# A turning product in halves, a decoding moved up, two decodes finished on another engine, and two smaller moves, in a retention, experts and gated-convolution kernel

## The chip, the cores and the metric

The kernel runs on 1 core of one Trainium2 chip. The metric is the device time of one execution in microseconds (us); lower is better. The core has five engines, each with its own instruction stream worked through in order: TensorE (PE; its weight loads are listed as PEld), VectorE (DVE), ScalarE (ACT), GpSimd (POOL) and SyncE (SP). They hand work to each other by semaphores. A `q` behind an engine's name marks an instruction of its sequencer, such as the issue of a DMA.

## The reference

Three layers follow one another, on 2 x 768 tokens of 512 columns.

```python
def _attn_ref(q, k, v):                       # 2 batches, 8 heads, 768 steps, 64 columns
    for t in range(S):
        state = gamma * state + einsum('bhd,bhe->bhde', k[:, :, t], v[:, :, t])
        y[:, :, t] = scale * einsum('bhd,bhde->bhe', q[:, :, t], state)

def _moe_ref(x, w_gate, w_local, w1, w2):     # 8 experts, 512 -> 1024 -> 512
    logits = x @ w_gate; local_gate = sigmoid(x @ w_local)
    for s in range(S):
        fresh_e = argmax(logits[b, s])
        e = fresh_e if s == 0 or local_gate[b, s] < 0.5 else prev_e
        p = softmax(logits[b, s])
        out[b, s] = p[e] * (maximum(x[b, s] @ w1[e], 0) @ w2[e])

def _moe2_ref(x, w_in, conv_w, w_out):        # 512 -> 1024 -> 512
    h = maximum(x @ w_in, 0)
    gate = sigmoid(conv over 3 tokens of h with conv_w)
    return (h * gate) @ w_out
```

`w_in`, `conv_w` and `w_out` arrive as 64-bit numbers, which the kernel itself turns into 32-bit ones.

## The kernel before, in words

The program is written by hand in the order in which every engine works. Its stages, with their times in the profiled execution:

**Attention, 0 to 61 us.** The 1536 tokens are cut into 12 tiles of 128. The step of the loop for tile `i` writes, in this order: `a_Z` (queries against the carried state, L362), the load of the next queries and keys, `a_X(i - 1)`, `logits` and `a_store` of the tile before, then `a_AV` (masked scores against the values, L374), `a_U` (the state, L396), and `a_S(i + 1)` (scores, L346). `a_X` (L406) is the turning product: it multiplies the attention's transposed result `xT` with `xw`, an identity of 128 columns with the 9 columns of the gates beside it, so that 137 columns come out with tokens on the partitions. There are four such products per tile, two into each of two banks. Each float32 product is two instructions in the trace. VectorE masks the scores (L352) and does the routing; ScalarE copies; GpSimd scales queries and values (L325, L332); SP loads three buffers ahead.

**Experts, 61 to 266 us** (`moe`). Weights are split into a high part (`whi`, ScalarE, L172) and a low part (`wlo`, VectorE, L181), and each product is made three times: high x high, low x high, high x low. A split unit is one such pair on 128x1024 numbers; behind its low part the next raw load is issued on SP. Tokens are gathered (`xg`, L611) and turned (`T`, with `xsh` on ScalarE, L584, and `xsl` on VectorE, L585). Experts 0 and 7 are done in two halves by `alone(e, half, ...)`, a generator that is advanced between other calls; experts 1 to 6 by `L1` (into `hh` and `hl`, L718 and L719) and `L2` (L744).

Two side works run in between:

- *Decoding.* Sixteen units of `w_in` and `w_out` (512 columns each) are turned from 64 to 32 bits. `dec_first` issues two ScalarE steps (L215, L216) on a loaded unit `draw`; `dec_second` does five VectorE operations (L218 to L224), two GpSimd ones (L226, L227, into `wdec`), and issues the next `draw` load on SP. `dec_first` finishes an open decoding first. The temporaries `dmag`, `df` and `ds` exist once; with `dec_first(mo)` the first two are `dmf` instead, in a ring of two.
- *The rest of the routing.* `route_rest` has five steps (L554 to L575) on 128x12 or 128x96 numbers: rows, `isov` to `posi`, `ex` with an exponential on ScalarE (L566), the reciprocal of its sum, and `G_all`. Each `next(rest, None)` does one.

`overflow` is a branch for tokens that no block holds. All engines pass it; what is written behind it can't run ahead of it.

**The joint between experts and the last layer, 245 to 266 us.** While `alone(7, 0)` and `alone(7, 1)` run on TensorE, the last two units are decoded, and the experts' results, stored by ScalarE as `ys` into `scr` (L689), are gathered back in token order by GpSimd (`c_gather`, L968), scaled with `G_all` (`c_scale`; VectorE L942, and ScalarE L944 for tile 4, whose buffer is `x_last`), turned by `c_T` (TensorE L950) and split (ScalarE L960, VectorE L963).

**The last layer, 266 us to the end.** `h2` (L993) and `o2` (L1045) keep TensorE busy; ScalarE and VectorE do the convolution and the gate.

Of the kernel before, what the change touches and what calls it, by code (L numbers as in the profile page):

```python
# [8 lines left out]
F32 = mybir.dt.float32  # L9
# [5 lines left out]
ALU = mybir.AluOpType  # L15
# [82 lines left out]
def tile_kernel(ctx: ExitStack, tc: tile.TileContext, consts, qk, kv, w1, w2, w_in, conv_w, w_out, out):  # L98
# [95 lines left out]
    n_dec = KD + KF // 2  # L194
    wdec = [(dp if j < n_dec - KEPT else cst).tile([P, 1024], F32, name=f"wdec{j}") for j in range(n_dec)]

    def decode(raw64, out, pool=None, s=None):

        n, m = out.shape
        r3 = raw64.rearrange("p (c two) -> p c two", two=2)  # L200
        lo, hi = r3[:, :, 0], r3[:, :, 1]

        def tmp(name, dt):
            return dp.tile([P, DM], dt, name=name, tag=name)[0:n, 0:m]

        if pool is None:
            mag, f = tmp("dmag", F32), tmp("df", F32)
        else:
            both = pool.tile([P, 2, DM], F32, name="dmf", tag="ow", bufs=2)
            mag, f = both[0:n, 0, 0:m], both[0:n, 1, 0:m]  # L210
        s = (tmp("ds", F32) if s is None else s[0:n, 0:m]).bitcast(I32)
        a = mag.bitcast(I32)
        ve = nc.vector

        nc.scalar.activation(out=mag, in_=hi.bitcast(F32), func=AF.Abs)  # L215
        nc.scalar.activation(out=f, in_=lo.bitcast(U32), func=AF.Copy, scale=2.0 ** -52)  # L216
        yield
        ve.tensor_scalar(mag, mag, F64_LOW, F64_HIGH, op0=ALU.max, op1=ALU.min)  # L218
        ve.tensor_scalar(a, a, 4, -2 ** 31, op0=ALU.logical_shift_left, op1=ALU.bitwise_xor)
        yield  # L220
        ve.tensor_scalar(s, hi, -2 ** 31, None, op0=ALU.bitwise_and)
        ve.scalar_tensor_tensor(out=a, in0=a, scalar=1, in1=s, op0=ALU.logical_shift_right, op1=ALU.bitwise_or)

        ve.tensor_scalar(s, a, -2 ** 23, None, op0=ALU.bitwise_and)  # L224
        yield
        nc.gpsimd.tensor_tensor(out=f, in0=f, in1=s.bitcast(F32), op=ALU.mult)  # L226
        nc.gpsimd.tensor_tensor(out=out, in0=f, in1=a.bitcast(F32), op=ALU.add)  # L227

    dec_src = []
    for dt in range(KD):  # L230
# [13 lines left out]
        queue.dma_start(out=t, in_=dec_src[u].bitcast(I32))  # L244
        dec_raw[u] = t

    def dec_first(pool=None, s=None):
        dec_second()
        u = dnx["run"]
        if u >= len(dec_src):  # L250
            return
        dnx["run"] += 1
        dec_raw["g"] = decode(dec_raw.pop(u), wdec[u // 2][:, (u % 2) * DM:(u % 2 + 1) * DM], pool, s)
        next(dec_raw["g"])

    def dec_second(queue=nc.sync):
        if "g" in dec_raw:
            for _ in dec_raw.pop("g"):
                pass
            dec_load(queue)  # L260
# [139 lines left out]
    def a_X(i):  # L400

        xT = xT_t.pop(i)
        x_t[i] = x2
        for p in range(NP):
            o = (p % 2) * P
            nc.tensor.matmul(x_t[i][p // 2][:, o:o + XN], lhsT=xT[:, p, :], rhs=xw[:, p, :],  # L406
                             start=(p % 2 == 0), stop=(p % 2 == 1), skip_group_check=True)

    def a_store(i):

# [192 lines left out]
    def moe(mo):  # L603
# [11 lines left out]
        def T(e, halves=(0, 1)):  # L615
            if e not in xs_t:
                xs_t[e] = (mo.tile([P, KD, CAP], F32R, name="xsh", tag="xsh", bufs=1),
                           mo.tile([P, KD, CAP], F32R, name="xsl", tag="xsl", bufs=1))
            for half in halves:
                sl = slice(half * P, (half + 1) * P)  # L620
                transposed(xg_t[e].pop(half), *(x[:, :, sl] for x in xs_t[e]))
# [73 lines left out]
        def L1(e):  # L695
            xh, xl = xs_t.pop(e)
            hh, hl = h_tiles(e)
            pb = [bank("b") if j < 3 else std for j in range(KF // 2)]
            for dt in range(KD):
                wh, wl = split[e * 8 + dt]  # L700
                if dt == 0:
                    dec_second()
                elif dt == 1:
                    next(rest, None)
                elif dt == 2:
                    dec_first(mo)
                for ft in range(KF):
                    o = pb[ft // 2][:, (ft % 2) * CAP + OFF:(ft % 2 + 1) * CAP]
                    fs = slice(ft * P, (ft + 1) * P)

                    for n, (a, b_) in enumerate(((wh, xh), (wl, xh), (wh, xl))):
                        nc.tensor.matmul(o, lhsT=a[:, fs], rhs=b_[:, dt, OFF:], start=(dt == 0 and n == 0 and ft % 2 == 0),  # L712
                                         stop=(dt == KD - 1 and n == 2), skip_group_check=True)
                    if dt == KD - 1 and ft % 2:
                        fp = ft // 2
                        dst = hh[:, 2 * fp:2 * fp + 2, OFF:]
                        pair = pb[fp].rearrange("p (a t) -> p a t", a=2)[:, :, OFF:]
                        nc.scalar.activation(out=dst, in_=pair, func=AF.Relu)  # L718
                        nc.vector.scalar_tensor_tensor(out=hl[:, 2 * fp:2 * fp + 2, OFF:], in0=pair, scalar=0.0,  # L719
                                                       in1=dst.bitcast(F32), op0=ALU.max, op1=ALU.subtract)  # L720
                split.pop(e * 8 + dt)
                if dt < KD - 1:
                    split_unit(nc.vector)
# [53 lines left out]
            pass  # L777
        rest = route_rest()
        for n, _ in enumerate(first):
            if n in (0, 1, 2, 5):  # L780
                split_unit(nc.vector)
            if n == 5:
                T(0, (1,))
            if n == 3:
                overflow(mo)
                gather(1)
            if n == 5:
                dec_first()
            elif n == 7:
                dec_second()  # L790
        for n, _ in enumerate(alone(0, 1, True)):
            if n == 0:
                dec_first()
            elif n == 1:
                dec_second()
            if n == 9:
                T(1, (0,))
            elif n == 11:
                T(1, (1,))
                gather(2)  # L800
# [10 lines left out]
        for n, _ in enumerate(alone(e, 0, False)):  # L811
            if n in (0, 8, 13):
                dec_second()
            elif n == 5:
                dec_first()
            elif n == 9:
                dec_first(mo, x0)
        raw0 = [dp.tile([P, 2, DM], F32, name="yg0", tag="draw", bufs=2) for _ in range(2)]
        ygs = [raw0[c // 2][:, c % 2, :] for c in range(4)] + [x_last.rearrange("p a t -> p (a t)"), x0]
        for c in range(NC):  # L820
# [2 lines left out]
        for n, _ in enumerate(alone(e, 1, True)):  # L823
            if 8 <= n < 12:
                c_scale(n - 8)
            if n == 7:
                window(1, [wp.tile([P, 1024], F32R, name="x2", tag=tag) for tag in ("whi", "whi", "wlo", "wlo")])
            if 10 <= n < 14:
                c_T(0, n - 10, "ab"[n % 2])
            if n == 12:  # L830
                c_scale(4)
            if n == 13:
                c_scale(5)

    def overflow(mo):
# [413 lines left out]
```

## Time and profile before

| | us |
|---|---|
| median of 3 timed runs | 410.25 |
| lowest and highest of them | 409.18, 411.04 |
| the profiled execution | 409.37 |
| its span (first to last instruction) | 407.6 |

| engine | busy us | share of the span |
|---|---|---|
| TensorE | 391.4 | 96% |
| VectorE | 286.8 | 70% |
| ScalarE | 246.6 | 60% |
| GpSimd | 117.8 | 29% |

The granted clock of TensorE was 0.996 over the span, where 1.00 is 2.4 GHz. TensorE is busy nearly everywhere, but its matmuls are pipelined, so that "busy" counts an instruction also while it waits behind the one before. What an instruction really takes is read from the distance between one's start and the next's. Of the other engines, only the places count at which TensorE waits for them. The chain of waits followed back from the last instruction lies on PE for 66% of the span, on DVE for 17%, on ACT for 6% and on DMA for 5%.

### The profile page before, as it was taken

How to read it: one execution, taken by the hardware profiler on the slowest of the kernel's cores; microseconds unless marked ns; L12 is line 12 of the kernel's file. 1: busy time of each engine (PE TensorE's matmuls, PEld its weight loads, DVE VectorE, ACT ScalarE, POOL GpSimd, SP SyncE). 2: the span in 40 equal slices, each digit the busy share in tenths (PEclk: the TensorE clock that was granted, in tenths of full speed). 3: DMA queues.
4: the chain of work that ended last, by engine and by line, in shares of the span. 5: the costliest groups of instructions: out<-in, count | busy, mean ns of one | idle time of the engine just before them, and what ended most of it. 6: DMA issues, size and time to landing. Idle time of an engine off the chain costs nothing.

```text
span 407.6 us, 7354 instructions
## 1 busy us (share of the span) xinstructions
PE 391.4 (96%) x2772; PEld 339.0 (83%) x2772; DVE 286.8 (70%) x544; ACT 246.6 (60%) x483; POOL 117.8 (29%) x110
## 2 busy tenths in 40 slices
PE   7999998979999999999999999799999999999996
PEld 4888876658989797998989777599979889998986
DVE  3368867957797999987877857659963736991350
ACT  4887752646855766576757563478864537981431
POOL 3455510264035153564744246532000000000000
PEclk9999999989999999999999999999999999999999
DMA  8999992868878797988979130533010010001002
GB/s 289 396 351 407 325 347 92 239 232 284 308 244 277 270 318 255 290 298 277 304 246 304 53 101 26 156 90 92 0 51 27 0 54 27 2 0 51 27 0 77
DMA packets 28087, 73.24 MB, mean 180 GB/s; under 512 B 3009, under 2 KB 3649, under 8 KB 28050
## 3 DMA queue, kind: packets, MB, share of 16 engines
q1 hardware_dynamic: 19506, 54.67, 39.1%
q10 hardware_dynamic: 6240, 10.55, 7.2%
q0 software_dynamic: 2304, 7.54, 6.0%
q8 instruction: 22, 0.36, 0.4%
q14 instruction: 15, 0.12, 0.1%
HBM read 62.26 MB, written 10.49 MB: 178 GB/s over the span
## 4 chain that ended last, share of the span: by engine, by line
PE 66%; DVE 17%; ACT 6%; DMA 5%; issue 4%; POOL 1%; ACTq 0%; DVEq 0%; POOLq 0%
PE c L1045 15%; PE b L993 11%; PE c L744 11%; DVE wlo L181 6%; PE rt L993 5%; PE b L712 4%; PE c L406 2%; PE b L652 2%; PE state L712 2%; PE rt L712 2%; PE b L346 2%; ACT whi L172 2%; DMA raw<-in_moe_w_dram 2%; PE a L374 2%; DMA C<-in_consts_dram 1%
## 5 line engine op out<-in xcount | busy, mean ns | idle before, releaser
L181 DVE TENSOR_TENSOR wlo<-raw,whi 128x1024 fp32r<-128x1024 f32 x64 | 82.1, 1295 | 18.4 <-ACT whi L172 17.6
L172 ACT CAST whi<-raw 128x1024 fp32r<-128x1024 f32 x64 | 66.7, 1055 | 40.6 <-PE c L744 21.9
L1012 DVE SCALAR_TENSOR_TENSOR cs<-hs,cw,cs 128x384 f32<-128x384 f32 x64 | 39.6, 619 | 30.6 <-ACT cs L1010 29.0
L226 POOL TENSOR_TENSOR dmf<-dmf,ds 128x512 f32<-128x512 f32 x12 | 24.9, 2076 | 83.5 <-DVE ds L224 50.1
L744 PE MATMUL c<-whi,hh 128*112 128x512 f32 x96 | 38.0, 395 | 0.3 <-ACT hh L718 0.3
L993 PE MATMUL b<-x,whi 128*128 128x386 f32 x176 | 37.1, 340 | 0.8 <-ACT x L960 0.8
L744 PE MATMUL c<-wlo,hh 128*112 128x512 f32 x96 | 37.5, 390 | 0.0
L1045 PE MATMUL c<-whi,gh 128*128 128x512 f32 x88 | 35.1, 399 | 0.0
L1045 PE MATMUL c<-whi,gl 128*128 128x512 f32 x88 | 34.9, 396 | 0.0
L1045 PE MATMUL c<-wlo,gh 128*128 128x512 f32 x88 | 34.7, 395 | 0.0
L993 PEld LDWEIGHTS b<-x,whi 128*128 128x128 f32 x176 | 31.2, 189 | 1.4 <-ACT x L960 1.2
L744 PE MATMUL c<-whi,hl 128*112 128x512 f32 x96 | 29.8, 392 | 0.6 <-DVE hl L719 0.6
L611 POOL DMA_INDIRECT xg<-scr,permi x15 | 20.3, 1353 | 26.5 <-DVE nbi L541 19.6
L712 PE MATMUL b<-xsl,whi 128*128 128x240 f32 x96 | 26.6, 277 | 0.4 <-DVE xsl L585 0.4
L712 PE MATMUL b<-xsh,whi 128*128 128x240 f32 x96 | 26.5, 276 | 0.0
L712 PE MATMUL b<-xsh,wlo 128*128 128x240 f32 x96 | 26.4, 275 | 0.0
L352 DVE TENSOR_TENSOR A<-b,mask 128x512 f32<-128x512 f32 x24 | 15.4, 685 | 11.1 <-PE b L346 11.1
L227 POOL TENSOR_TENSOR wdec<-dmf 128x512 f32<-128x512 f32 x13 | 22.8, 1757 | 1.0
L1016 ACT ACTIVATE sg<-cs 128x384 f32<-128x384 f32 x32 | 16.6, 519 | 9.1 <-DVE gl L1022 8.5
L744 PEld LDWEIGHTS c<-whi,hl 128*112 128x112 f32 x96 | 17.2, 181 | 5.8 <-DVE hl L719 1.5
L744 PEld LDWEIGHTS c<-whi,hh 128*112 128x112 f32 x96 | 17.4, 181 | 4.9 <-ACT hh L718 0.6
L744 PEld LDWEIGHTS c<-wlo,hh 128*112 128x112 f32 x96 | 17.4, 181 | 4.2
(251 smaller groups left out, 1015.9 us busy)
## 6 DMA issues: line engine op xcount, KB each, us to landing
raw<-in_moe_w_dram SPq DMA_DIRECT2D x64, 512.0 KB, 4.8
qk<-in_qk_dram SPq DMA_DIRECT2D x11, 512.0 KB, 6.6
kv<-in_kv_dram SPq DMA_DIRECT2D x11, 512.0 KB, 6.6
draw<-in_moe_w_in_dram SPq DMA_DIRECT2D x8, 512.0 KB, 3.6
draw<-in_moe_w_out_dram SPq DMA_DIRECT2D x8, 512.0 KB, 3.3
scr<-xo ACTq DMA_DIRECT2D x11, 256.0 KB, 8.1
out_dram<-os ACTq DMA_DIRECT2D x11, 256.0 KB, 2.0
scr<-ys ACTq DMA_DIRECT2D x10, 256.0 KB, 4.2
```

The costliest lines, as they stand in the source:

```text
L172: nc.scalar.copy(hi, raw[u])
L181: engine.tensor_tensor(out=lo, in0=t, in1=hi.bitcast(F32), op=ALU.subtract)
L226: nc.gpsimd.tensor_tensor(out=f, in0=f, in1=s.bitcast(F32), op=ALU.mult)
L227: nc.gpsimd.tensor_tensor(out=out, in0=f, in1=a.bitcast(F32), op=ALU.add)
L352: nc.vector.tensor_tensor(out=A_t[i][j], in0=sc2[j].rearrange("p (a t) -> p a t", a=NP), in1=mask.unsqueeze(1).to_broadcast([P, NP, P]), o ...
L611: nc.gpsimd.indirect_dma_start(out=t, out_offset=None, in_=xrow, in_offset=bass.IndirectOffsetOnAxis(ap=permi[:, col:col + 1], axis=0))
L712: nc.tensor.matmul(o, lhsT=a[:, fs], rhs=b_[:, dt, OFF:], start=(dt == 0 and n == 0 and ft % 2 == 0), stop=(dt == KD - 1 and n == 2), skip ...
L744: nc.tensor.matmul(yp[t][0:P - o], lhsT=a[:, ft, t * P + o:(t + 1) * P], rhs=b_[:, ws], start=(ft == 0 and a is hh and b_ is wh), stop=(ft ...
L993: nc.tensor.matmul(pb[:, 0:WN], lhsT=split[u_in + dt][wi][:, fs], rhs=x_[dt // 2][:, dt % 2, :], start=(n == 0), stop=(n == 3 * KD - 1))
L1012: nc.vector.scalar_tensor_tensor(out=cs, in0=tap[j], scalar=cw[:, j, ft:ft + 1], in1=cs, op0=ALU.mult, op1=ALU.add)
L1016: nc.scalar.activation(out=sg, in_=cs, func=AF.Sigmoid)
L1045: nc.tensor.matmul(ops[t][:, 0:n_], lhsT=a[:, ts_], rhs=b_[:, ws], start=(ft == 0 and n == 0), stop=(ft == KF - 1 and n == 2))
```

## The change

Five edits:

1. `a_X` makes each product as two: 64 columns of `xT` into the lower half of the partitions, then 64 into the upper half.
2. The first decoding after `overflow`: `dec_first` stands at step 3 of `alone(0, 0)`, not 5; `dec_second` at step 4, not 7; the split unit of step 5 at step 7. The turning `T(0, (1,))` stays at step 5.
3. `route_rest` is advanced in `L2` alone, so its five steps fall into experts 1 to 5 instead of 1 to 3.
4. The last two decodings end on VectorE: the operations of L226 and L227 leave GpSimd.
5. `c_scale(4)`, ScalarE's, stands behind `c_T(0, 3)` instead of ahead of it.

```diff
+    def decode(raw64, out, pool=None, s=None, last=nc.gpsimd):
...
-        nc.gpsimd.tensor_tensor(out=f, in0=f, in1=s.bitcast(F32), op=ALU.mult)
-        nc.gpsimd.tensor_tensor(out=out, in0=f, in1=a.bitcast(F32), op=ALU.add)
+        last.tensor_tensor(out=f, in0=f, in1=s.bitcast(F32), op=ALU.mult)
+        last.tensor_tensor(out=out, in0=f, in1=a.bitcast(F32), op=ALU.add)
...
         for p in range(NP):
             o = (p % 2) * P
-            nc.tensor.matmul(x_t[i][p // 2][:, o:o + XN], lhsT=xT[:, p, :], rhs=xw[:, p, :],
-                             start=(p % 2 == 0), stop=(p % 2 == 1), skip_group_check=True)
+            for half in HALF:
+                nc.tensor.matmul(x_t[i][p // 2][half, o:o + XN], lhsT=xT[:, p, half], rhs=xw[:, p, :],
+                                 start=(p % 2 == 0), stop=(p % 2 == 1), skip_group_check=True)
...
                 if dt == 0:
                     dec_second()
-                elif dt == 1:
-                    next(rest, None)
                 elif dt == 2:
                     dec_first(mo)
...
-            if n in (0, 1, 2, 5):
+            if n in (0, 1, 2, 7):
                 split_unit(nc.vector)
-            if n == 5:
-                T(0, (1,))
             if n == 3:
                 overflow(mo)
                 gather(1)
-            if n == 5:
                 dec_first()
-            elif n == 7:
+            elif n == 4:
                 dec_second()
+            elif n == 5:
+                T(0, (1,))
...
             elif n == 5:
-                dec_first()
+                dec_first(last=nc.vector)
             elif n == 9:
-                dec_first(mo, x0)
+                dec_first(mo, x0, nc.vector)
...
                 c_T(0, n - 10, "ab"[n % 2])
-            if n == 12:
+            if n == 13:
                 c_scale(4)
-            if n == 13:
                 c_scale(5)
```

In the order of instructions, TensorE in one tile of the attention before (`c_79` and `c_80` are X's two banks, `a_75` and `a_76` those of Z and A·V; x2 counts products):

```order
L362 MATMUL a_75<-qk,Z_106 64x128
L362 MATMUL a_76<-qk,Z_106 64x128
L406 MATMUL c_79<-xw,xT 128x137 x2
L406 MATMUL c_80<-xw,xT 128x137 x2
L374 MATMUL a_75<-A_300,kv 64x128 x2
L374 MATMUL a_76<-A_301,kv 64x128 x2
```

And the same tile with the change:

```order
L362 MATMUL a_75<-qk,Z_106 64x128
L362 MATMUL a_76<-qk,Z_106 64x128
L407 MATMUL c_79<-xw,xT 64x137 x4
L407 MATMUL c_80<-xw,xT 64x137 x4
L374 MATMUL a_75<-A_304,kv 64x128 x2
L374 MATMUL a_76<-A_305,kv 64x128 x2
```

Nothing moves; two products of a bank have become four, in the array shape that A·V has.

VectorE behind the branch of `overflow` before:

```order
L181 TENSOR_TENSOR wlo<-raw,whi 128x1024
L585 TENSOR_TENSOR xsl<-a_76,xsh 128x4x128
L218 TENSOR_SCALAR dmag<-dmag 128x512
L219 TENSOR_SCALAR dmag<-dmag 128x512
L221 TENSOR_SCALAR ds<-draw 128x512
L222 SCALAR_TENSOR_TENSOR dmag<-dmag,ds 128x512
L224 TENSOR_SCALAR ds<-dmag 128x512
L687 COPY ys<-c_79 128x512
```

And with the change:

```order
L218 TENSOR_SCALAR dmag<-dmag 128x512
L219 TENSOR_SCALAR dmag<-dmag 128x512
L221 TENSOR_SCALAR ds<-draw 128x512
L222 SCALAR_TENSOR_TENSOR dmag<-dmag,ds 128x512
L224 TENSOR_SCALAR ds<-dmag 128x512
L586 TENSOR_TENSOR xsl<-a_76,xsh 128x4x128
L181 TENSOR_TENSOR wlo<-raw,whi 128x1024
L688 COPY ys<-c_79 128x512
```

The five operations of the decoding have passed the split and `xsl`, and the split now follows `xsl`. On ScalarE the two steps of the decoding have likewise passed `whi` and `xsh`.

VectorE in the joint before (`x_108` is the buffer `x0`):

```order
L224 TENSOR_SCALAR ds<-dmag 128x512
L218 TENSOR_SCALAR dmf<-dmf 128x512
L219 TENSOR_SCALAR dmf<-dmf 128x512
L221 TENSOR_SCALAR x_108<-draw 128x512
L222 SCALAR_TENSOR_TENSOR dmf<-dmf,x_108 128x512
L224 TENSOR_SCALAR x_108<-dmf 128x512
L644 TENSOR_TENSOR hl<-a_75,hh 128x4x128
```

And with the change:

```order
L224 TENSOR_SCALAR ds<-dmag 128x512
L226 TENSOR_TENSOR df<-df,ds 128x512
L227 TENSOR_TENSOR wdec_93<-df,dmag 128x512
L218 TENSOR_SCALAR dmf<-dmf 128x512
L219 TENSOR_SCALAR dmf<-dmf 128x512
L221 TENSOR_SCALAR x_108<-draw 128x512
L222 SCALAR_TENSOR_TENSOR dmf<-dmf,x_108 128x512
L224 TENSOR_SCALAR x_108<-dmf 128x512
L226 TENSOR_TENSOR dmf<-dmf,x_108 128x512
L227 TENSOR_TENSOR wdec_93<-dmf 128x512
L645 TENSOR_TENSOR hl<-a_75,hh 128x4x128
```

Four operations have come to VectorE, two behind each decoding; on GpSimd the gathers of L968 now follow the decoding before these two directly.

## Rows read from the trace of the kernel before

**Rows 1.** Chain of waits: start us, us, what (a run of instructions counts as one).

```profile
11.67 1.14 PE c L406 x8
...
253.73 4.50 DMA yg<-scr,posi
```

**Rows 2.** Windows: stretch, length, busy (count) of PE, PEld, DVE, ACT, POOL; PEclk; DMA share; GB/s.

```profile
36.00:46.00 10.00, 9.75 (x160) 8.27 (x160) 9.31 (x30) 7.16 (x22) 5.22 (x8) 1.00 1.01 374
87.40:90.40 3.00, 3.00 (x8) 2.17 (x7) 2.61 (x3) 1.80 (x3) 2.43 (x2) 0.50 0.53 175
257.00:258.00 1.00, 0.00 (x0) 0.00 (x0) 0.00 (x0) 0.00 (x0) 0.70 (x2) 1.00 0.65 221
```

**Rows 3.** Timeline of PE in one attention tile: start us, us, engine, line, operation, tiles.

```profile
20.23 1.21 PE L406 MATMUL c<-xw,xT 128*128 128x137 f32 x8
21.37 1.09 PE L374 MATMUL a<-A,kv 128*64 128x128 f32 x16
22.29 0.63 PE L396 MATMUL state<-kv 128*64 128x64 f32 x16
```

**Rows 4.** Timeline of PE around the first decoding; in brackets idle before it, and releaser.

```profile
79.40 0.50 PE L652 MATMUL b<-whi,xsl 128*128 128x512 f32 x1
...
86.38 0.66 PE L640 MATMUL a<-ident,hr 128*128 128x128 f32 x4 [2.99 <-ACT hr L663]
```

**Rows 5.** Timelines of DVE, POOL and ACT around the first decoding.

```profile
77.52 1.23 DVE L181 TENSOR_TENSOR wlo<-raw,whi 128x1024 fp32r<-128x1024 f32 x1 [0.21 <-ACT xsh L584]
...
81.71 0.68 DVE L687 COPY ys<-c 128x512 f32<-128x512 f32 x1
...
83.33 1.26 POOL L227 TENSOR_TENSOR wdec<-df,dmag 128x512 f32<-128x512 f32 x1
...
84.62 0.66 ACT L215 ACTIVATE dmag<-draw 128x512 f32<-128x512 f32 x1 [5.98 <-POOL wdec L227]
```

**Rows 6.** Timelines of ACT and PE in experts 2 and 3.

```profile
128.37 0.28 ACT L566 ACTIVATE ex<-ex 128x96 f32<-128x96 f32 x1 [4.74 <-DVE ex L565]
...
132.20 0.48 PE L744 MATMUL c<-whi,hh 128*112 128x512 f32 x1 [0.34 <-ACT hh L718]
...
133.56 0.49 PE L744 MATMUL c<-whi,hl 128*112 128x512 f32 x1 [0.18 <-DVE hl L719]
...
156.89 0.48 PE L744 MATMUL c<-whi,hl 128*112 128x512 f32 x1 [0.45 <-DVE hl L719]
```

**Rows 7.** Timeline of POOL in expert 1, beside a split of VectorE.

```profile
117.59 2.15 POOL L226 TENSOR_TENSOR dmf<-dmf,ds 128x512 f32<-128x512 f32 x1 [19.93 <-issue]
```

**Rows 8.** Timelines of the joint: DVE, ACT, POOL and PE.

```profile
246.75 1.40 DVE L219 TENSOR_SCALAR dmf<-dmf 128x512 int32<-128x512 int32 x1
...
252.81 0.69 DVE L644 TENSOR_TENSOR hl<-a,hh 128x512 fp32r<-128x512 f32 x1 [2.04 <-ACT hh L643]
...
255.60 0.69 DVE L644 TENSOR_TENSOR hl<-a,hh 128x512 fp32r<-128x512 f32 x1 [0.61 <-ACT hh L643]
...
248.17 0.33 ACTq L689 DMA_DIRECT2D scr<-ys  x1
...
264.92 0.73 ACT L944 ACTIVATE x_last<-x_last,G_all 128x512 f32<-128x512 f32 x1
...
252.28 1.30 POOL L227 TENSOR_TENSOR wdec<-dmf 128x512 f32<-128x512 f32 x1
...
258.76 2.02 POOL L968 DMA_INDIRECT x_last<-scr,posi  x1 [0.30 <-issue]
...
258.79 0.66 PE L950 MATMUL a<-ident,yg 128*128 128x128 f32 x4 [2.46 <-DVE yg L942]
...
265.76 0.96 PE L993 MATMUL b<-x,whi 128*128 128x386 f32 x4 [0.81 <-ACT x L960]
```

**Rows 9.** Page, DMA issues: tiles, engine, operation, count, KB each, us from issue to landing.

```profile
out_dram<-os ACTq DMA_DIRECT2D x11, 256.0 KB, 2.0
scr<-ys ACTq DMA_DIRECT2D x10, 256.0 KB, 4.2
```

More of the change, by code (lines that the diff above doesn't have):

```diff
@@ L195, in tile_kernel @@
     wdec = [(dp if j < n_dec - KEPT else cst).tile([P, 1024], F32, name=f"wdec{j}") for j in range(n_dec)]
-    def decode(raw64, out, pool=None, s=None):
+    def decode(raw64, out, pool=None, s=None, last=nc.gpsimd):
         n, m = out.shape
@@ L245, in dec_load, with dec_first @@
         dec_raw[u] = t
-    def dec_first(pool=None, s=None):
+    def dec_first(pool=None, s=None, last=nc.gpsimd):
         dec_second()
@@ L252, in dec_first @@
         dnx["run"] += 1
-        dec_raw["g"] = decode(dec_raw.pop(u), wdec[u // 2][:, (u % 2) * DM:(u % 2 + 1) * DM], pool, s)
+        dec_raw["g"] = decode(dec_raw.pop(u), wdec[u // 2][:, (u % 2) * DM:(u % 2 + 1) * DM], pool, s, last)
         next(dec_raw["g"])
```

## The prediction, made before the result

> **What bounds the kernel now.** I read the chain of waits first, then the timelines of the stretches that the edits touch, and the windows last. The profiled execution took 409.37 us, of which the span is 407.6. From about 266 us to the end, TensorE is dense in the output network and no edit reaches that far, so whatever is won or lost before 266 us arrives at the end in full. The question is who ends last in five places.
>
> In the attention the turning product (X, line 406) is itself on the chain in eight of the eleven tiles that the loop turns (the first of these pieces stands in [rows 1]). In the other three, around 32 to 47 us, VectorE is busy 9.31 of 10 us and the DMA engines are full (share 1.01) [rows 2]. In the mixture of experts TensorE is dense with four kinds of exception: 2.99 us before 86.38 for ScalarE's relu `hr` [rows 4], three short waits in experts 2 and 3 [rows 6], 2.46 us before 258.79 for the first gathered rows, and 0.81 us before 265.76 for a cast [rows 8].
>
> **1. X in halves.** Four products of 128x137 (eight instructions, since each float32 product is two) become eight products of 64x137, sixteen instructions. X takes 1.14 us now, from 20.23 to 21.37. The nearest row is A·V right behind it: also eight products on 64 columns, sixteen instructions of 128 elements, in 0.92 us (21.37 to 22.29) [rows 3]. Scaled by 137/128 that is 0.985 us, so 0.155 us less per tile. Each of A·V's instructions starts 0.0575 us after the one before, which is only possible if the two halves run side by side. Eight tiles on the chain give 8 x 0.155 = 1.24 us. In the three tiles bound by VectorE I count nothing, and I round to **-1.3** for X and A·V having one array shape less between them. Bounds: 0, if loads become the bound at once, and -1.7, if all eleven tiles gain.
>
> X's sixteen rows are about as long as A·V's, so A·V already carries whatever the issue of twice the instructions costs. The Trainium skill, "TensorEngine Tiling (Array Packing)", section "Instruction Overhead", speaks against this edit: about 60 cycles of overhead for each matmul, and the advice not to take the tiling from a dimension that is already small. As an estimate from that page, eight more instructions at 60 cycles of 2.4 GHz are 0.2 us a tile, more than the gain, and the sum would be 1.3 us smaller by it; A·V's 0.0575 us for a whole instruction [rows 3] is why I don't go by it.
>
> **2. First decoding moved up (77 to 97 us).** Now the second decode's first ScalarE step (84.62) waits 5.98 us for GpSimd's `wdec` of the first (83.33 + 1.26) [rows 5], and the relu that TensorE needs stands behind it on ScalarE. Hence TensorE's 2.99 us [rows 4]. Afterwards the granted clock is 0.50 from 87.4 to 90.4 [rows 2], the 1.2 GHz level; the same products at 2.4 GHz would take half of those 3.0 us, so the slow clock costs 1.5 us.
>
> In the changed order VectorE runs the five decode operations ahead of `xsl`, and the split `wlo` (1.23) behind it. The five now lie between the end of `xsl`, just before TensorE's product on it at 79.40 [rows 4], and `ys` at 81.71 [rows 5]: about 2.35 us. `xsl` is then 2.35 - 1.2 = 1.15 us later, and TensorE waits that long at this product: a new wait of about 1.2 us. GpSimd starts about as much earlier as the split and `xsl` no longer stand ahead of the decode, 1.8 us, but the moved `wlo` now runs beside its two steps, and beside such a VectorE operation a GpSimd step took 2.15 us [rows 7] instead of 1.30 [rows 8]. So `wdec` is ready 0.7 to 1.7 us earlier, and TensorE goes on at 84.7 to 85.7 instead of 86.38; I take 85.2, **-1.2** net of the new wait, which lies inside it. Two waits of about 1.2 and 0.5 us then stand for one of 2.99. After a wait of 2.46 us the clock was still 1.00 [rows 2, 8], so I expect it to hold: -1.5. Against that, ScalarE does one `whi` ahead of the next relu, which I put at +0.3 to +0.5. Sum **-2.2**. Bounds: 0 (the wait only changes its place and the clock falls anyway) and -3.2 (1.7 + 1.5). SP's one raw load now stands behind the draw load, and the moved split unit is for expert 1, whose products begin only after 96 us: nothing.
>
> **3. Routing's rest later.** The step with the exponential sits on ScalarE at 128.37 after a wait of 4.74 us, and the splits and `hh` of expert 2 are behind it; the products for it waited 0.34 and 0.18 us, those of expert 3, where the last step runs ahead of two splits on VectorE, 0.45 us [rows 6]. In the new order no step stands in L1, so both neighbours disappear from those places. All three waits go: **-1.0**. The steps then land in experts 4 and 5, where TensorE does not wait. Bounds: 0, if a step in expert 2's L2 delays the same splits, and -1.3, with the restart after each wait.
>
> **4. Last two decodes finished by VectorE (tail).** The first gather (GpSimd) starts at 253.73 because `wdec` runs to 253.58, lands 4.50 us later [rows 1, 8], VectorE scales, TensorE turns at 258.79. After the change GpSimd is free, and the gather waits only for what it reads: the store of `ys`, issued 248.17 [rows 8]. Stores of this size landed in 2.0 or 4.2 us by the medians of two such stores [rows 9], so the gather can start between 250.2 and 252.4 and land between 254.7 and 256.9. Next late is then VectorE's order: the scaling stands behind `hl` at 255.60 + 0.69 [rows 8]. That puts TensorE at about 256.8: **-1.95**; with the slow store, which the gather's rows reach 0.6 us later, -1.3. The four operations added to VectorE are of the shape of `hl` (two inputs, 128x512), 0.69 us [rows 8], together 2.8 us. One of its decode operations now takes 1.40 us beside GpSimd and would shorten, and the 2.04 us in which it idles before 252.81 cover most of the rest [rows 8]. Without the shortening, 0.7 us of it would fall on the `hl` at 252.81.
>
> **5. One scaling behind the casts.** ScalarE's 0.73 us on `x_last` (264.92) stands ahead of the casts for which TensorE waits 0.81 before 265.76 [rows 8]. Moved behind them, the cast can start as soon as its transposes allow: **-0.55**; bounds 0 and -0.73. The store of `ys` behind it starts a little later, and nothing reads it soon.
>
> **Sum.** -1.3 - 2.2 - 1.0 - 1.95 - 0.55 = -7.0 us, 402.4 by the profiled execution. The median of the three timed runs is 410.25, 0.9 higher, which would make 403.25. I take the middle, **402.8 us**.
>
> **Rivals.**
> A. *Attention bound by its loads.* For it: a DMA share of 1.01 over ten microseconds [rows 2]. Against: X is on the chain in eight tiles with TensorE busy before and after. It takes part 1 away: 404.1.
> B. *The first decoding only trades its wait*: the clock falls again, or `xsl` costs what `hr` gave back. For it: the new wait of 1.2 us is certain by the order. Against: both waits together are shorter than the one now. Takes part 2 away: 405.0.
> C. *Gathers late.* The issue of the gather at 258.76, beside a VectorE split, took 2.02 us [rows 8], and the four new VectorE operations stand just ahead of the first gather. The Trainium skill, "SBUF — State Buffer", section "SBUF: two separate sides", has a rule by which this would come: VectorE and GpSimd share a port pair as an exclusive lock, and GpSimd that is locked out cannot write the descriptors of its DMAs; the 2.02 us agrees with it. Two new operations of 0.69 that hold the first gather up, and the slow store, cost 1.4 us, over half of part 4: 404.2.
> D. *Slower: the halves of X do not run side by side.* Then sixteen instructions of 1.14/8 = 0.1425 us take 2.28 us, 1.14 more per tile, in eight to eleven tiles +9.1 to +12.5, against 5.7 of the other parts: 413.7 to 417.1 by the median. It decides from 0.7 us more per tile. For it: nothing but that X's operand is wider. Against: A·V [rows 3].
> That an edit does nothing is no case of its own: the order of instructions shows all five.
>
> **Chances.** The forecast 0.62 (400.5 to 404), A 0.08, B 0.10, C 0.08, two or three of these together 0.07 (405.5 to 410, counted as within 0.5%), D 0.05. A difference under 0.5% (2.05 us, from 408.2 to 412.3) is about what a measurement of this kernel can't tell from no change; nearly three parts must fail for it. All bounds together reach from -9.3 (1.7 + 3.2 + 1.3 + 2.4 + 0.7) to 0; against the median that is 401.0 at the low end, against the lower profiled execution 400.1, and upward the range takes in A, B, C and the nearer half of their pairs: 400.0 to 406.3. Faster 0.88, same 0.07, slower 0.05.
>
> **What would show it.** Part 1: X at about 0.99 us per tile, the first A·V that much closer. Part 2: TensorE waiting about 1.2 us for `xsl` near 78 us and under 1 us for `hr`, and no slice at 0.50. Part 3: no wait over 0.1 us on `hh` and `hl` in experts 2 and 3. Part 4: first gather before 252.5 minus the earlier gains, TensorE waiting under 1 us for it. Part 5: the wait before the first output product under 0.3 us. Wrong would be X above 1.14 us, a clock of 0.50 in 80 to 90 us, or a new wait for VectorE between 110 and 235 us.

## The result: 404.63 us, and the profile after

The changed kernel takes 404.63 us (median of 4 runs, 404.07 to 404.94) against 409.72 us of the kernel before in the runs beside it. The ratio is 0.9875, with a 95% interval from 0.9856 to 0.9893: 5.1 us faster, where 7 were forecast. The sign and the range held; the gain was a quarter smaller. The result lies just outside the forecast's own bin (400.5 to 404).

Where it went is read from the starts of the same products in TensorE's two timelines. The table gives the distance between such starts, in us, in the profiled executions (409.37 and 404.4); what the prediction expected stands in the last column:

| stretch | before | after | difference | forecast |
|---|---|---|---|---|
| start to last tile's X | 60.76 | 60.79 | 0.0 | -1.3 (part 1) |
| to expert 1's first product | 35.93 | 33.73 | -2.2 | -2.2 (part 2) |
| experts 1 to 3 | 70.30 | 69.51 | -0.8 | -1.0 (part 3) |
| experts 4 to 6, and to the first turned `hr` of expert 7 | 72.17 | 72.50 | +0.3 | 0 |
| to the first output product | 26.60 | 24.20 | -2.4 | -2.5 (parts 4, 5) |
| to the last product | 138.39 | 138.46 | +0.1 | 0 |

**X in halves**, the timeline of PE in the tile of [rows 3]:

```profile
19.98 1.16 PE L407 MATMUL c<-xw,xT 128*64 128x137 f32 x16
20.98 1.09 PE L374 MATMUL a<-A,kv 128*64 128x128 f32 x16
21.85 0.34 PE L396 MATMUL state<-kv 128*64 128x64 f32 x5
```

X takes 1.00 us from its start to A·V's, as forecast (0.985), and A·V 0.87 instead of 0.92. The two halves do run side by side, and the overhead per instruction that the prediction set aside does not show. And yet the last tile's X starts when it did.

**The first decoding**, PE, DVE and POOL, against [rows 4, 5]:

```profile
80.73 0.50 PE L653 MATMUL b<-whi,xsl 128*128 128x512 f32 x1 [1.30 <-DVE xsl L586]
...
85.53 0.66 PE L641 MATMUL a<-ident,hr 128*128 128x128 f32 x4 [0.82 <-ACT hr L664]
...
80.59 1.99 DVE L181 TENSOR_TENSOR wlo<-raw,whi 128x1024 fp32r<-128x1024 f32 x1
...
81.58 2.16 POOL L227 TENSOR_TENSOR wdec<-df,dmag 128x512 f32<-128x512 f32 x1
```

Two waits of 1.30 and 0.82 us stand for the one of 2.99. The split and GpSimd's step beside it stretch each other, from 1.23 and 1.26 us [rows 5] to 1.99 and 2.16. The clock, in the window of [rows 2] (same columns), stays at its upper level:

```profile
87.40:90.40 3.00, 2.95 (x18) 2.21 (x17) 2.47 (x3) 2.25 (x4) 2.92 (x2) 1.00 0.46 146
```

**Experts and joint**, PE and POOL, against [rows 6, 8]:

```profile
153.93 0.49 PE L743 MATMUL c<-whi,hl 128*112 128x512 f32 x1 [0.36 <-DVE hl L718]
...
248.44 1.46 POOL L965 DMA_INDIRECT yg<-scr,posi  x1 [8.48 <-DVE dmf L226]
...
254.10 0.33 PE L947 MATMUL a<-ident,yg 128*128 128x128 f32 x1 [0.41 <-DVE yg L939]
...
260.73 0.44 PE L990 MATMUL b<-x,whi 128*128 128x386 f32 x1 [0.20 <-ACT x L957]
```

The waits of expert 2 are gone; that of expert 3 has stayed, at 0.36 for 0.45 us. The first gather now starts 5.3 us earlier (248.44 for 253.73), of which 2.6 us are the lead that TensorE already has at expert 7's first turned `hr` (236.53 for 239.16). TensorE waits 0.41 for its rows instead of 2.46, and 0.20 instead of 0.81 for the cast.

### The profile page after: what moved, and what is told of

Its sections match the earlier page's. It is cut to its first block, busy times and chain, and to the rows that moved or that the text cites. A ratio compares the mean times of both kernels' runs of the same rounds, so it can differ in the third digit from the quotient of the medians.

```text
span 402.6 us, 7552 instructions
## 1 busy us (share of the span) xinstructions
PE 388.7 (97%) x2868; PEld 336.9 (84%) x2868; DVE 295.2 (73%) x548; ACT 245.9 (61%) x483; POOL 111.5 (28%) x106
## 4 chain that ended last, share of the span: by engine, by line
PE 53%; DVE 13%; DMA 6%; issue 4%; ACT 3%; POOL 0%; ACTq 0%; DVEq 0%
PE c L1042 15%; PE b L990 12%; PE c L743 8%; DVE wlo L181 7%; PE rt L990 5%; DMA raw<-in_moe_w_dram 5%; PE b L711 3%; PE b L653 2%; ACT whi L172 2%; DVE hl L718 2%; DMA xg<-scr,permi 1%; PE c L672 1%; PE state L711 1%; PE rt L711 1%; DVE xsl L586 1%
## 5 line engine op out<-in xcount | busy, mean ns | idle before, releaser
L181 DVE TENSOR_TENSOR wlo<-raw,whi 128x1024 fp32r<-128x1024 f32 x64 | 87.1, 1381 | 12.0 <-ACT whi L172 11.3
L172 ACT CAST whi<-raw 128x1024 fp32r<-128x1024 f32 x64 | 66.6, 1057 | 41.0 <-PE c L743 18.9
L226 POOL TENSOR_TENSOR dmf<-dmf,ds 128x512 f32<-128x512 f32 x12 | 24.9, 2075 | 83.5 <-DVE ds L224 59.6
L227 POOL TENSOR_TENSOR wdec<-dmf 128x512 f32<-128x512 f32 x12 | 20.7, 1722 | 0.9
```

The lines of the kernel that those rows point to most:

```text
L172: nc.scalar.copy(hi, raw[u])
L181: engine.tensor_tensor(out=lo, in0=t, in1=hi.bitcast(F32), op=ALU.subtract)
L226: last.tensor_tensor(out=f, in0=f, in1=s.bitcast(F32), op=ALU.mult)
L227: last.tensor_tensor(out=out, in0=f, in1=a.bitcast(F32), op=ALU.add)
```

## The experiments

Theories: **(add)** the five parts add up as the prediction's sum has them; **(load)** rival A, the attention's loads take X's gain; **(DVE)** VectorE takes it between 30 and 47 us; **(chain)** the parts in the middle depend on each other, since expert 2's splits start from a raw load that doesn't come earlier with TensorE.

All profiles answer to one table, distances of starts in us as above (the way from the first X to the last is split at the 1st, 5th, 9th and 12th tile's X; what lies ahead of the first X, 11.5 to 11.9 us, is left out). Each row is one execution:

| kernel | X 1 to 5 | X 5 to 9 | X 9 to 12 | to expert 1 | experts 1 to 3 | 4 to `hr` of 7 | to output |
|---|---|---|---|---|---|---|---|
| before | 18.10 | 18.24 | 12.82 | 35.93 | 70.30 | 72.17 | 26.60 |
| after | 17.55 | 18.87 | 12.62 | 33.73 | 69.51 | 72.50 | 24.20 |
| x_only | 17.55 | 19.03 | 12.62 | 34.63 | 71.80 | 72.18 | 26.41 |
| dec_only | 18.10 | 18.23 | 12.82 | 33.65 | 71.10 | 72.17 | 26.82 |
| rest_only | 18.10 | 18.24 | 12.82 | 35.92 | 68.68 | 72.53 | 26.33 |
| no_rest | 17.56 | 18.19 | 12.64 | 33.56 | 71.44 | 72.18 | 24.20 |
| tail_only | 18.10 | 18.25 | 12.82 | 34.57 | 70.29 | 72.17 | 24.80 |
| scale_only | 18.09 | 18.37 | 12.82 | 35.90 | 69.71 | 72.17 | 26.04 |
| no_x | 18.10 | 18.24 | 12.82 | 33.66 | 69.20 | 72.48 | 24.18 |
| l2_dve | 17.56 | 18.37 | 12.62 | 33.87 | 68.64 | 72.17 | 24.33 |
| few_kv | 18.10 | 18.24 | 12.82 | | | | |
| few_kv_x | 18.72 | 18.05 | 12.62 | | | | |
| no_lo | 18.09 | 18.09 | 12.81 | 35.23 | 70.14 | 72.17 | 26.46 |
| no_lo_x | 17.56 | 18.29 | 12.62 | 36.42 | 71.04 | 72.17 | 26.50 |

### X in halves: x_only and no_x

x_only is the kernel before with the first edit alone:

```diff
-            nc.tensor.matmul(x_t[i][p // 2][:, o:o + XN], lhsT=xT[:, p, :], rhs=xw[:, p, :],
-                             start=(p % 2 == 0), stop=(p % 2 == 1), skip_group_check=True)
+            for half in HALF:
+                nc.tensor.matmul(x_t[i][p // 2][half, o:o + XN], lhsT=xT[:, p, half], rhs=xw[:, p, :],
+                                 start=(p % 2 == 0), stop=(p % 2 == 1), skip_group_check=True)
```

> The kernel before with the halves of X alone. The prediction's term expects -1.3 us (408.4 where before is at 409.7). Its rival A, attention bound by loads, expects X at 0.99 us per tile in the trace and yet 0.0, within 0.3 us, since GpSimd's scaling waits for the same loads at about 46.7 us as before. If the halves cost something where small products stand ahead of X (0.33 us has become 0.42 there), at most +0.3.

Measured: 409.56 against 409.51 us, ratio 0.9997 (0.9981 to 1.0014). no_x is the changed kernel without that edit (the same diff turned round).

> The changed kernel with X as four whole products again. The prediction's term expects it 1.3 us slower, 405.9. If the gain is lost within the attention, as the halves alone showed: 404.6, within 0.4 us, and if the halves gain in those executions in which no load is late, up to 0.7 us slower.

Measured: 404.02 us, ratio to before 0.9865 (0.9850 to 0.9881), where the changed kernel has 0.9875 (0.9856 to 0.9893). So the halves are worth nothing that can be measured, alone or with the rest. The table's first three columns say why: where whole products stand, the three stretches are 18.1, 18.1 to 18.4 and 12.8 us in every profile. Halves give 0.55 in the first (but for few_kv_x, below) and 0.20 in the last. In the middle the stretch is between 0.2 us shorter and 0.8 longer than before, which can take all of it back. The interval of x_only reaches to 0.8 us faster: it leaves out the -1.3 of part 1, but not a gain of some tenths in the executions whose middle is short (from the first X to the last 48.39 us in no_rest and 48.55 in l2_dve, against 49.16 before, 49.04 in the changed kernel and 49.20 in x_only).

### What takes it back: few_kv, few_kv_x, no_lo, no_lo_x

few_kv leaves out three of the attention's loads; few_kv_x has X in halves besides.

```diff
+FEW = (4, 6, 8)
...
+        if i in FEW:
+            kv_t[i] = kv_t[i - 1]
+            return
         t = ld.tile([P, 2, H, D], F32, name="kv", tag="kv", bufs=3)
...
     def a_scale_v(i):
-        if i >= NT:
+        if i >= NT or i in FEW:
             return
```

> The kernel before, but tiles 4, 6 and 8 of the attention take the keys and values of the tile before instead of loading and scaling their own (three loads of 512 KB less; the attention's result is another one). If the loads bind the attention: the last tile's X starts well over 1 us before 60.8. If VectorE binds it between 30 and 47 us: within 0.3 us of 60.8. The total depends on how the other result is routed, so only the pair with the next kernel is compared.

> The same with X in halves. If the loads took the gain of the halves, and no longer bind here: 0.8 to 1.6 us before few_kv, at the last tile's X and in the total. If VectorE or the end of the attention took it: the same as few_kv within 0.3 us.

The window of the middle tiles in few_kv (columns as in [rows 2]) and its last tile's X on PE:

```profile
36.00:46.00 10.00, 9.73 (x162) 8.28 (x160) 9.31 (x30) 6.01 (x18) 4.74 (x7) 1.00 0.87 317
...
60.80 0.38 PE L410 MATMUL c<-xw,x_last 128*128 128x137 f32 x1 [0.39 <-ACT x_last L387]
```

The DMA share falls from 1.01 to 0.87 and nothing moves: 60.80 for 60.76. So leaving out three loads gains nothing: they do not bind the kernel **before**. With halves on top the middle stretch gives 0.19 us, the best of all profiles, but its first stretch is 1.2 us longer than with halves elsewhere, of which 0.55 is a pause of TensorE at 26.1 us that nothing in the profile explains; the totals are equal (467.9 and 468.01 us, both long because the other result is routed into the `overflow` branch, whose products stand near 84 us in both profiles).

no_lo takes the splits from VectorE instead:

```diff
             t, hi = raw.pop(u), split[u][0]
+            if not load:
+                split[u] = (hi, hi[:, :])
+                return
             lo = wp.tile([P, 1024], F32R, name="wlo", tag="wlo")
```

> The kernel before without VectorE's five low-part splits during the attention (1.22 us each; the products with these low parts take the high part instead, so the first weights are less exact). Leaving out three loads had moved nothing in the attention. If VectorE binds the stretch from 30 to 47 us: the last tile's X starts 2 to 3.6 us before 60.8, until TensorE or the loads become the bound. If it was TensorE or the loads all the while: within 0.3 us of 60.8.

> The same with X in halves. If VectorE's splits took the gain of the halves in the middle tiles: 0.9 to 1.4 us before no_lo at the last tile's X, of it some 0.5 in the first five tiles. If the loads take it as soon as VectorE does not: 0 to 0.4 us, and GpSimd waiting over 1 us for queries between 30 and 50 us.

```profile
36.00:46.00 10.00, 9.92 (x162) 8.37 (x162) 6.73 (x27) 7.16 (x22) 4.38 (x8) 1.00 1.00 387
...
60.60 0.50 PE L409 MATMUL c<-xw,x_last 128*128 128x137 f32 x2 [0.38 <-ACT x_last L386]
```

VectorE falls from 9.31 to 6.73 us busy and the last X comes 0.15 to 0.2 us earlier. So VectorE, busy as it was, held up next to nothing: the chain of waits had shown its splits there, but TensorE is busy 9.75 of 10 us with them [rows 2] and 9.92 without. In time no_lo has 0.9979 (0.9967 to 0.9992) and no_lo_x 0.9984 (0.9968 to 1.0000) of the kernel before: the halves give nothing here either. Both theories that I had of the middle tiles fall for the kernel before. With halves, though, waits appear there or grow (the only one before is 0.25 us for VectorE's logits, at 40.33), in no_lo_x for ScalarE's copies (first two rows), in the changed kernel for VectorE's logits and in both for late loads (POOL):

```profile
32.79 1.20 PE L410 MATMUL c<-xw,xT 128*64 128x137 f32 x16 [0.25 <-ACT xT L386]
36.83 0.67 PE L365 MATMUL a<-qk,Z 64*64 64x128 f32 x16 [0.38 <-ACT Z L401]
```

```profile
40.55 0.34 PE L478 MATMUL rt<-ident,far 1*128 1x1 f32 x3 [0.85 <-DVE LG L441]
...
37.55 1.28 POOL L325 TENSOR_TENSOR qk<-qk,wdec 128x512 f32<-128x512 f32 x1 [1.44 <-DMA qk<-in_qk_dram]
```

By these waits TensorE, the loads, VectorE and ScalarE end there within some tenths of each other, so that a shorter TensorE meets the next at once. With halves the middle stretch is 18.05 us where loads were left out (few_kv_x), 18.2 to 18.4 in no_rest, no_lo_x and l2_dve, and 18.9 to 19.0 in the changed kernel and x_only. GpSimd's waits for loads between 28 and 40 us go with it, but don't order it: 4.3 us in the changed kernel, 1.9 in x_only, 2.9 in l2_dve, 0.4 before. What orders it is where a late load puts GpSimd's scaling of the queries. Where that runs beside a short step of VectorE, the step ends only after it, and TensorE waits for it or for what follows (0.35 us at 31.91 in x_only, 0.85 at 40.55 in the changed kernel). DVE and POOL of x_only, then DVE of the changed kernel, whose POOL row stands above:

```profile
30.34 1.51 DVE L507 TENSOR_SCALAR sl<-slot,R 128x256 f16<-128x256 f16 x3
...
29.75 1.27 POOL L325 TENSOR_TENSOR qk<-qk,tq 128x512 f32<-128x512 f32 x1 [1.67 <-DMA qk<-in_qk_dram]
...
38.19 0.68 DVE L218 TENSOR_SCALAR dmag<-dmag 128x24 f32<-128x24 f32 x1
```

In no_rest, whose attention is written like the changed kernel's, these steps take 0.68 and 0.17 us. VectorE's short steps are stretched by 0.83 us in x_only, by 0.67 in the changed kernel (0.51 here and 0.16 at 34.77), by 0.17 in l2_dve and not in no_rest, and the middle stretches are 0.84, 0.68 and 0.18 us longer than no_rest's. The sizes fit to 0.01 us; no run varied this alone.

The end of the attention gives nothing either: from the 11th X to the 12th it is 3.35 us before and 3.34 after, because the 12th waits for ScalarE's `x_last` (0.39 before, 0.58 after), which comes no earlier.

### The middle: dec_only, rest_only, no_rest

dec_only has the second edit alone, rest_only the third alone; no_rest is the changed kernel with the third undone.

```diff
-            if n in (0, 1, 2, 5):
+            if n in (0, 1, 2, 7):
                 split_unit(nc.vector)
-            if n == 5:
-                T(0, (1,))
             if n == 3:
                 overflow(mo)
                 gather(1)
-            if n == 5:
                 dec_first()
-            elif n == 7:
+            elif n == 4:
                 dec_second()
+            elif n == 5:
+                T(0, (1,))
```

> The kernel before with the first decoding moved up alone. If the parts simply add up: -2.2 us, as the start of expert 1 moved in the changed kernel. If expert 2's splits don't follow TensorE (a raw load issued at 96.4 took 8.2 us in the changed kernel, and the split behind it began a microsecond later than before although TensorE was 2.2 us ahead), the three waits in experts 2 and 3 grow and it gives -0.8 to -1.5.

```diff
                 if dt == 0:
                     dec_second()
-                elif dt == 1:
-                    next(rest, None)
                 elif dt == 2:
```

> The kernel before with routing's rest moved alone. The prediction's term expects -1.0 us, the changed kernel's trace -0.45 if the parts add up. If the splits of expert 3, stretched to 1.9 us beside GpSimd in its L1, set the last of the three waits, that wait stays near 0.4 us, the two in expert 2 go, and it gives -0.5 to -0.8.

> The changed kernel with routing's rest put back where it was. If the parts add up: 0.45 us slower than the changed kernel, so 405.1. If the moved steps are what lets experts 2 and 3 keep up with a TensorE that is 2.2 us ahead: 1.2 to 2.0 us slower, 405.8 to 406.6, with waits of over a microsecond in expert 2.

Measured: dec_only 0.9952 (0.9933 to 0.9971), so -2.0 us; rest_only 0.9958 (0.9942 to 0.9973), so -1.7; no_rest 405.21 us, 0.9892 (0.9869 to 0.9916), 0.6 above the changed kernel's median, a difference inside the intervals.

The times go with (add): dec_only was expected at -2.2 by it and at -0.8 to -1.5 by (chain), though its interval, -1.2 to -2.7, takes in both; no_rest was expected at 405.1 by it and at 405.8 to 406.6 by (chain). The five edits alone, x_only, dec_only, rest_only and the two of the next section, make about -5.5 us together, where the whole change makes -5.1; the difference is inside the intervals.

The table seems to say (chain): dec_only reaches expert 1 2.28 us earlier, but experts 1 to 3 take 0.80 longer. PE and ACT of dec_only, then PE of x_only:

```profile
130.87 0.49 PE L744 MATMUL c<-whi,hh 128*112 128x512 f32 x1 [1.17 <-ACT hh L718]
...
104.62 1.05 ACT L172 CAST whi<-raw 128x1024 fp32r<-128x1024 f32 x1 [0.75 <-DMA raw<-in_moe_w_dram]
...
132.61 0.48 PE L745 MATMUL c<-whi,hh 128*112 128x512 f32 x1 [1.33 <-ACT hh L719]
```

The wait for `hh` is 1.17 instead of 0.34 us [rows 6]. The chain of waits goes back from this `hh` over VectorE's and ScalarE's splits to a raw load issued at 96.46 us that took 8.08. But the same wait stands in x_only and no_lo_x (1.17), where the decoding has not moved, and tail_only reaches expert 1 1.36 us earlier than before and loses none of it (70.29). The six profiles with the old order of decoding and routing have 69.7 to 71.8 us in experts 1 to 3, so one profile of dec_only can't show a loss of 0.80.

What the wait does go with is that load. In the eight profiles with the routing's steps where they were, it took 7.7 to 8.8 us in dec_only, no_rest, x_only and no_lo_x, with a wait for `hh` of 1.17 to 1.36, and 6.7 to 7.3 us in before, tail_only, scale_only and no_lo, with a wait of at most 0.34. With the steps moved (the changed kernel, rest_only, no_x, l2_dve) TensorE never waits for this `hh`, although the load takes 7.9 to 8.4 us in three of them. So part 3 takes away a wait that is long when the load is late. The long load stands in all five profiles with the decoding moved up and in two of seven without: part 2 may make it more likely, but that (chain) costs part 2 a fixed share of its gain is not shown. Undoing part 3 in the changed kernel makes experts 1 to 3 longer by 1.93 us, and part 3 alone shortens them by 1.62; the two differ by less than executions of the same order do.

### The joint: tail_only, scale_only

```diff
             elif n == 5:
-                dec_first()
+                dec_first(last=nc.vector)
             elif n == 9:
-                dec_first(mo, x0)
+                dec_first(mo, x0, nc.vector)
```

> The kernel before with the last two decodes finished by VectorE alone. The prediction's term expects -1.95 us (-1.3 with the slow store), the changed kernel's trace -2.07 between the start of the last expert and the first turned rows; rival C, gathers held up by VectorE, expects under -0.8 and a gather's issue of 2 us among the first two.

```diff
-            if n == 12:
-                c_scale(4)
             if n == 13:
+                c_scale(4)
                 c_scale(5)
```

> The kernel before with the one scaling moved behind the casts alone. The prediction's term expects -0.55 us and a wait of 0.2 instead of 0.81 before the first output product. If it is the late gather of these rows that makes the wait (it was 0.16 to 0.19 in two kernels that kept this order but came there at another time), the gain is 0 to -0.3, or the wait comes back in another place.

tail_only: 0.9960 (0.9944 to 0.9975), -1.6 us; the last column falls by 1.80. scale_only: 0.9997 (0.9981 to 1.0012) in time, 0.56 in the last column; an effect of half a microsecond is inside that interval. PE in tail_only and then in scale_only:

```profile
255.28 0.66 PE L950 MATMUL a<-ident,yg 128*128 128x128 f32 x4 [0.41 <-DVE yg L942]
...
262.52 0.80 PE L993 MATMUL b<-x,whi 128*128 128x386 f32 x3 [0.80 <-ACT x L960]
```

```profile
258.52 0.66 PE L949 MATMUL a<-ident,yg 128*128 128x128 f32 x4 [2.51 <-DVE yg L941]
...
264.88 0.45 PE L992 MATMUL b<-x,whi 128*128 128x386 f32 x1 [0.19 <-ACT x L959]
```

Each edit takes its own wait and leaves the other's, and 1.80 + 0.56 = 2.36 is nearly the 2.40 of both. Rival C does not show: in the changed kernel gathers beside VectorE took up to 1.71 us to issue (the first 1.46), and TensorE still waits only 0.41 us for its rows.

### A further step: l2_dve

In the changed kernel the wait of expert 3 follows three splits that take 5.68 us beside GpSimd's two steps. l2_dve lets VectorE finish those decodings too that end at the start of an L1:

```diff
                 elif j == 3:
-                    dec_first(mo)
+                    dec_first(mo, None, nc.vector)
```

> The changed kernel with those decodings of experts 1 to 6 finished by VectorE that begin in L2 and end at the start of the next L1. There three splits take 1.9 us each beside GpSimd, ahead of the low part that TensorE waits for. If this sharing makes the two waits left in experts 3 and 4 (0.36 and 0.07 us, 0.65 with what each restart costs): 0.4 to 0.7 us faster than the changed kernel, 404.0 to 404.2. If VectorE's own two operations (1.4 us) cost more than the stretching: the waits grow, 405 or more.

Measured: 403.21 us (402.37 to 403.69), ratio to before 0.9840 (0.9823 to 0.9857). DVE of the changed kernel, then of l2_dve:

```profile
147.63 5.68 DVE L181 TENSOR_TENSOR wlo<-raw,whi 128x1024 fp32r<-128x1024 f32 x3
```

```profile
146.98 0.69 DVE L226 TENSOR_TENSOR dmf<-dmf,ds 128x512 f32<-128x512 f32 x1
147.70 0.69 DVE L227 TENSOR_TENSOR wdec<-dmf 128x512 f32<-128x512 f32 x1
148.31 3.49 DVE L181 TENSOR_TENSOR wlo<-raw,whi 128x1024 fp32r<-128x1024 f32 x3
```

VectorE pays 1.38 us for its own two operations and gets back 2.19. No product waits in experts 2 to 6 any more, and experts 1 to 3 and 4 to 6 fall to 68.64 and 72.17 us. It is 1.4 us below the changed kernel's median, where 0.7 was the most that was expected; the two expert columns of the profiles give 1.2, and the two intervals just touch. It beats the kernel before clearly and is the best version that was run.

## Why the prediction was right, and where it was not

**Part 1, -1.3, was wrong: 0.** The duration was right (0.985 said, 1.00 measured), and so was the step that the halves run side by side. The step that failed is "eight tiles on the chain give 8 x 0.155". It took a product's presence on the chain of waits for a gain in full. Three things were missed. In the middle tiles, counted at zero, the halves can lose: up to 0.8 us, which a term that ends at 0 had no room for. At the end, the last tile's X waits for `x_last`, which comes no earlier. And where a small turned column stands between Z and X, X starts 0.42 instead of 0.33 us behind it, so that the distances on both sides of such a tile gain 0.05 to 0.1 us instead of 0.20. Rival A, with its chance of 0.08, named the right outcome, and its mechanism only in part: late loads take the gain of the halved kernel in some executions, by way of GpSimd and VectorE, and do not bind the kernel before.

**Part 2, -2.2, was right at its place, by terms that cancel.** The new wait is 1.30 us (1.2 said), the second 0.82 (0.5). TensorE goes on at 85.53 (85.2 said), which is -0.85 instead of -1.2. The clock held: the next `hr` follows after 2.78 us instead of 4.04, -1.26 instead of -1.5. The +0.3 to +0.5 for ScalarE's `whi` did not come: from there to expert 1 it is 6.21 us, 6.27 before. The clock's share is not there in every execution: x_only and tail_only, with the old order and without a fall, reach expert 1 1.3 us sooner than before; but nearly all executions of the kernel before have a fall somewhere (last section). And the reason for "so I expect it to hold" does not bear it: the window of [rows 2] at 257 lies inside the wait, where the clock was still 1.00 ahead of the fall at 87 us too. Behind that wait it did hold, but in dec_only and rest_only the wait at the same place was followed by a fall.

**Part 3, -1.0, was mis-sized.** Alone it gives 1.62 in experts 1 to 3 and -1.7 us in time: the three waits are 0.97 us, and the rest lies around them, as the term's own bound (-1.3, with the restart after each wait) allowed for in part. In the changed kernel 0.8 is left against the kernel before, because a wait of 0.36 us stays in expert 3. In rest_only that wait is gone, as the term has it; in the changed kernel, where TensorE comes earlier, the splits beside GpSimd keep it, and l2_dve, which frees them, takes it away. "TensorE does not wait in experts 4 and 5" failed by 0.3 us in the fourth column of the changed kernel and of rest_only; in l2_dve that too is gone.

**Parts 4 and 5, -2.5, were right**: -2.4, by the steps as told. VectorE's order behind `hl` sets TensorE's start: `hl`, scaling, then the product at 254.10, which with TensorE's lead of 2.6 us is the 256.8 of the prediction. The slow store did not come.

**The rivals.** The time alone does not choose: 404.63 lies between C's 404.2 and B's 405.0, with A's 404.1 close by. The profiles choose A's outcome. B and D did not come: the clock held, and X got shorter. C cost nothing that shows.

## What to carry to other kernels

Shortening an engine's work pays only as far as the next engine is late. Where four resources end within tenths of each other, as in the middle tiles here, a shorter product gave nothing that could be measured, even though it did all that was hoped. Before a loss in one profile is put down to an edit, look for the same loss in profiles without it: experts 1 to 3 differed by 2 us between kernels with the same order there, and the loss went with a load that came late in some of them. Moving work out of the way of such a load took the wait away, late or not. And where two engines stretch each other, the total of both is what a move between them should be judged by.

## What the runs showed of the hardware

**The clock's fall is not settled by the wait ahead of it.** With the old order of the decoding TensorE stood about 3 us near 86 us in these profiles. In five of them (before, rest_only, scale_only, no_lo, no_lo_x) the way from there to the next `hr`, nine products, then took 4.0 to 4.8 us, in x_only and tail_only 2.8. The window in x_only:

```profile
87.40:90.40 3.00, 2.94 (x16) 2.19 (x15) 2.71 (x4) 2.25 (x4) 2.17 (x2) 1.00 0.55 176
```

So the 1.25 us that the clock costs near [rows 2]'s window are there in some executions and not in others. With the new order all five profiles took 2.8 us.

A second place is the wait for the first gathered rows. After 2.46 us of it the clock stayed at 1.00 in the kernel before, but in dec_only and rest_only it fell to the 1.2 GHz level after 2.44 and 1.93 us. The window in dec_only:

```profile
257.80:260.80 3.00, 3.00 (x12) 2.52 (x11) 2.85 (x6) 1.77 (x4) 2.57 (x2) 0.50 0.52 138
```

The mean granted clock of each execution shows how often: it was 0.996 or lower in 62 of the 64 executions of the kernel before that stand beside the experiments, in 4 of 7 of dec_only and in 5 of 12 of tail_only. In all 18 executions of the four kernels that have both edits (the changed kernel, no_rest, no_x, l2_dve) it was 0.998 or higher.

**An equal load took 3.3 to 8.2 us**: raw loads of 512 KB landed 3.3 us after the issue at 89.46 and 8.17 after that at 96.43 in the changed kernel. GpSimd issues gathers from 92.96 to 97.2 us, beside the second; that they make it late is not shown.

**Two engines that share cost both**: three splits took 5.68 us beside two GpSimd steps, and 3.49 without them; the GpSimd steps took 2.15 us each, and 1.3 alone [rows 8]. In the middle tiles a VectorE step of 0.17 us that began at 38.19 beside GpSimd's scaling (37.55 to 38.83) ended at 38.87. The Trainium skill, "SBUF — State Buffer", section "SBUF: two separate sides", describes an exclusive lock between VectorE and GpSimd; the stretching of both agrees with it.
